# A two-dimensional DFT and a gated feed-forward block: three edits to the weight preparation in the first batch

## The chip, the cores and the metric

The kernel runs on one core of a Trainium2 chip. The metric is the device time of one execution in microseconds (us), median of several runs.

## What is computed

The real part of a two-dimensional DFT over sequence (3008) and width (256) of each of 8 batches, then a feed-forward block of width 2048 with a piecewise gate:

```python
X = np.fft.fft(np.fft.fft(x, axis=1), axis=2).real      # x: 8 x 3008 x 256
h = X @ w_in                                            # 256 x 2048
g = np.where(h >= 1, h, np.where(h <= -1, 0.0, (h + 1) ** 2 / 4))
out = g @ w_out                                         # 2048 x 256
```

The weights arrive as 64-bit floats, and the kernel has to turn their bits into fp32 itself.

## The kernel before

The sequence DFT is split into two stages (`stage1`, `stage2`, with `nyquist` for one column of the width DFT); the width DFT is folded into w_in, so that h comes from one matrix product. All products of the feed-forward block are made in three passes over high and low parts (`wh`, `wl`, `pqh`, `pql`, `gh`, `gl`, `woh`, `wol`).

A **unit** is one block of 128 columns of w_in for one of three column chunks of one batch (16 blocks x 3 chunks x 8 batches). `gemm1` of a unit gives two banks `uv` on TensorE (L359, 6 matmuls); VectorE makes `us` and the two halves of `h` (L362, L364, L365); ScalarE a Relu and a Square into `a` (L372, L373); VectorE the gate (L374); ScalarE its copy `gh` (L375); POOL the rest `gl` (L378). `gemm2` of a unit comes LAG = 4 units later in the code and adds 12 matmuls into four `acc` banks (L402). In batch 0 each chunk has two visits of 8 units: the first ends with the sums copied from `acc` to `o` (L412 on ScalarE, L414 on VectorE) and sent to DRAM, the second adds them. All other batches have one visit of 16 units.

Batch 0 also has to prepare the weights while it runs. There are 16 blocks of weights, **conversions** 0 to 15 (`convert_w`, step "c"): four groups of two blocks of w_in and two of w_out. Conversions 6 to 15 work in the loaded tile `raw` and one PSUM bank `cps`: ScalarE scales the low word into `cps` (L208), VectorE masks the mantissa (L217), adds (L218) and shifts out the exponent (L221), ScalarE takes the exponent's Relu (L222), VectorE its minimum with 255 and the shift to its place (L223), the sign (L224) and the product (L225). Conversions 0 to 5 use other tiles. A **fold** (`fold_w_in` and `fold_delta`, steps "f" and "d") multiplies two converted blocks of w_in by the DFT matrices (L246, L255) and splits the result into `wh` and `wl` (L169, L170). Folds 2 and 3 take their banks from the pool `uv`, which has three and also serves `gemm1`, so the next unit's `gemm1` stands behind them. Units 0 to 7, 8 to 15 and 16 to 23 are the first visits of the three chunks; unit 24 is the first that needs fold 2.

A table `STEPS` says ahead of which unit each preparation step is written. From there a scheduler sets the order on each engine by its own costs and priorities; each engine then runs its queue in order. The FFT of batch 1 starts at unit 25 (FIRST_DFT); POOL adds the two halves of its input x into `y` (L131), which has three buffers, before TensorE's `stage1` matmuls (L270), and ScalarE empties those into `z` (L280).

The lines that the steps of the prediction touch most:

```python
        nc.vector.tensor_scalar(shifted, exp, 255.0, float(1 << 23), op0=ALU.min, op1=ALU.mult)
```

## Time and profile before

| | us |
|---|---|
| median of 3 runs (1764.12 to 1766.73) | 1764.72 |
| the profiled execution | 1765.38 |
| its span | 1763.6 |
| TensorE busy | 1735.8 (98%) |
| VectorE busy | 1440.0 (82%) |
| ScalarE busy | 1346.3 (76%) |
| POOL busy | 1202.1 (68%) |

PE is TensorE's matmuls, DVE is VectorE, ACT is ScalarE, POOL is GpSimd. A share of busy time over the whole span hides that the stretches differ; the rows below are therefore read by stretch. A line number is one of the kernel before.

### The profile page before, as it was taken

How to read it: one execution, taken by the hardware profiler on the slowest of the kernel's cores; microseconds unless marked ns; L12 is line 12 of the kernel's file. 1: busy time of each engine (PE TensorE's matmuls, PEld its weight loads, DVE VectorE, ACT ScalarE, POOL GpSimd, SP SyncE). 2: the span in 40 equal slices, each digit the busy share in tenths (PEclk: the TensorE clock that was granted, in tenths of full speed). 3: DMA queues.
4: the chain of work that ended last, by engine and by line, in shares of the span. 5: the costliest groups of instructions: out<-in, count | busy, mean ns of one | idle time of the engine just before them, and what ended most of it. 6: DMA issues, size and time to landing. Idle time of an engine off the chain costs nothing.

```text
span 1763.6 us, 21942 instructions
## 1 busy us (share of the span) xinstructions
PE 1735.8 (98%) x7982; PEld 1420.5 (81%) x7982; DVE 1440.0 (82%) x1766; ACT 1346.3 (76%) x1580; POOL 1202.1 (68%) x838
## 2 busy tenths in 40 slices
PE   9988999999999999999999999999999999999998
PEld 6766888888888788888888888888888888888877
DVE  6999788888887888878888788878888788888887
ACT  5777877777777877777778877788778787777776
POOL 1545966776768766787667876677676766667775
PEclk9999999999999999999999999999999999999999
DMA  7013321010010100110001100011000000000000
GB/s 230 12 66 101 101 104 60 28 50 30 13 51 28 53 30 1 51 48 33 30 10 51 50 28 24 22 39 50 28 24 34 1 23 32 11 25 5 19 25 24
DMA packets 29963, 72.51 MB, mean 41 GB/s; under 512 B 2976, under 2 KB 8224, under 8 KB 29856
## 3 DMA queue, kind: packets, MB, share of 16 engines
q1 hardware_dynamic: 29568, 70.08, 12.1%
q8 instruction: 62, 1.02, 0.2%
q10 hardware_dynamic: 288, 1.05, 0.2%
q14 instruction: 45, 0.37, 0.1%
HBM read 43.31 MB, written 27.81 MB: 40 GB/s over the span
## 4 chain that ended last, share of the span: by engine, by line
PE 61%; ACT 10%; POOL 9%; issue 6%; DVE 5%; ACTq 0%; POOLq 0%; DVEq 0%
PE acc L402 38%; PE uv L359 19%; POOL gl L378 9%; DVE h L374 4%; ACT a L373 4%; ACT gh L375 3%; ACT a L372 3%; PE s L270 2%; PE s L309 2%; ACT z L280 1%; DVE o L414 0%; DVE h L365 0%; DVE h L364 0%; POOL y L131 0%; ACT o L412 0%
## 5 line engine op out<-in xcount | busy, mean ns | idle before, releaser
L378 POOL TENSOR_TENSOR gl<-h,gh 128x512 fp32r<-128x512 f32 (+1 forms) x765 | 1095.1, 1454 | 513.3 <-ACT gh L375 491.7
L374 DVE SCALAR_TENSOR_TENSOR h<-a,h 128x1024 f32<-128x1024 f32 (+1 forms) x385 | 578.0, 1502 | 219.7 <-ACT a L373 218.1
L375 ACT ACTIVATE gh<-h 128x1024 fp32r<-128x1024 f32 (+1 forms) x385 | 400.6, 1041 | 356.9 <-DVE h L374 344.2
L402 PE MATMUL acc<-gh,woh 128*128 128x512 f32 (+1 forms) x1536 | 608.3, 396 | 6.7 <-ACT gh L375 3.3
L402 PE MATMUL acc<-gl,woh 128*128 128x512 f32 (+1 forms) x1536 | 604.6, 394 | 9.1 <-POOL gl L378 9.1
L402 PE MATMUL acc<-gh,wol 128*128 128x512 f32 (+1 forms) x1536 | 596.2, 388 | 0.0
L372 ACT ACTIVATE a<-h,biases 128x1024 f32<-128x1024 f32 (+1 forms) x385 | 431.7, 1122 | 10.0 <-DVE h L365 7.7
L373 ACT ACTIVATE a<-a 128x1024 f32<-128x1024 f32 (+1 forms) x385 | 398.8, 1036 | 7.1
L402 PEld LDWEIGHTS acc<-gl,woh 128*128 128x128 f32 x1536 | 288.8, 188 | 76.4 <-POOL gl L378 16.8
L402 PEld LDWEIGHTS acc<-gh,woh 128*128 128x128 f32 x1536 | 289.3, 188 | 68.9 <-DVE o L414 5.5
L402 PEld LDWEIGHTS acc<-gh,wol 128*128 128x128 f32 x1536 | 289.5, 188 | 59.2
L364 DVE TENSOR_TENSOR h<-us,uv 128x512 f32<-128x512 f32 (+1 forms) x384 | 259.3, 675 | 67.2 <-POOL gl L378 27.3
L359 PE MATMUL uv<-pqh,wh 128*128 128x512 f32 (+1 forms) x768 | 303.7, 395 | 3.0 <-DVE us L362 2.9
L359 PE MATMUL uv<-pql,wh 128*128 128x512 f32 (+1 forms) x768 | 301.4, 392 | 0.0
L359 PE MATMUL uv<-pqh,wl 128*128 128x512 f32 (+1 forms) x768 | 299.5, 390 | 0.0
L362 DVE SCALAR_TENSOR_TENSOR us<-nyb,delta,uv 128x512 f32<-128x512 f32 (+1 forms) x384 | 278.5, 726 | 14.6 <-PE uv L359 13.8
L365 DVE TENSOR_TENSOR h<-us,uv 128x512 f32<-128x512 f32 (+1 forms) x384 | 256.0, 667 | 0.0
L359 PEld LDWEIGHTS uv<-pqh,wh 128*128 128x128 f32 x768 | 144.4, 188 | 40.9 <-DVE us L362 6.8
L359 PEld LDWEIGHTS uv<-pql,wh 128*128 128x128 f32 x768 | 144.6, 188 | 32.1
L359 PEld LDWEIGHTS uv<-pqh,wl 128*128 128x128 f32 x768 | 144.4, 188 | 30.5 <-issue 0.2
L131 POOL TENSOR_TENSOR y<-x 96x512 f32<-96x512 f32 x60 | 106.4, 1774 | 20.0 <-DMA x<-in_x_dram 8.2
L280 ACT ACTIVATE z<-s 64x192 f32<-64x192 f32 x256 | 86.6, 338 | 6.5 <-PE s L275 1.7
(54 smaller groups left out, 548.0 us busy)
## 6 DMA issues: line engine op xcount, KB each, us to landing
x<-in_x_dram SPq DMA_DIRECT2D x64, 384.0 KB, 3.3
out_dram<-o SPq DMA_DIRECT2D x30, 512.0 KB, 2.8
out_dram<-o SPq DMA_DIRECT2D x16, 482.0 KB, 3.0
nyb<-nyr SPq DMA_DIRECT2D x24, 256.0 KB, 3.4
raw<-in_moe_w_out_dram SPq DMA_DIRECT2D x8, 512.0 KB, 10.9
raw<-in_moe_w_in_dram SPq DMA_DIRECT2D x6, 512.0 KB, 4.5
part<-o SPq DMA_DIRECT2D x4, 512.0 KB, 3.2
o<-part SPq DMA_DIRECT2D x4, 512.0 KB
```

The source lines that it names most:

```text
L131: nc.gpsimd.tensor_tensor(y, t[:, 0], t[:, 1], op=ALU.add)
L280: nc.scalar.activation(dst, src, AF.Copy)
L359: nc.tensor.matmul(t[:, :n], w[m][:, cols], r[:, m, :n], start=(j == 0), stop=(j == 2))
L362: nc.vector.scalar_tensor_tensor(us, nyb[b, k][:, :n], delta[:, f : f + 1], uv[0], op0=ALU.mult, op1=ALU.add)
L364: nc.vector.tensor_tensor(h[:, 0], us, uv[1], op=ALU.subtract)
L365: nc.vector.tensor_tensor(h[:, 1], us, uv[1], op=ALU.add)
L372: nc.scalar.activation(a[:, sl], h[:, sl], AF.Relu, bias=half, scale=0.5)
L373: nc.scalar.activation(a[:, sl], a[:, sl], AF.Square)
L374: nc.vector.scalar_tensor_tensor(h[:, sl], a[:, sl], 1.0, h[:, sl], op0=ALU.min, op1=ALU.max)
L375: nc.scalar.activation(gh[:, sl], h[:, sl], AF.Copy)
L378: eng.tensor_tensor(gl[:, sg], h[:, sg], gh[:, sg].bitcast(F32), op=ALU.subtract)
L402: nc.tensor.matmul(acc[:, :n], w[:, f, wc], g[:, sg], start=(first and j == 0), stop=(last and j == 2))
```

## The change

Three edits. First, in conversions 6 to 15 the minimum with 255 and its scaling by 2^23 go from one VectorE instruction to two ScalarE activations: Relu(255 - e) in place in `raw`, then 255 * 2^23 - 2^23 times it into `cps`; conversions 0 to 5 keep the VectorE instruction. A third constant, 255, joins the biases. Second, all four copies of the sums at the end of a first visit are ScalarE's; before, VectorE took two of them. Third, fold 2 is written ahead of unit 14 and not 13, while conversion 10 and the load of block 12 stay at 13.

```diff
--- before.py
+++ after.py
@@ -79,7 +79,8 @@
     6: "o7 l10",
     9: "c8",
     11: "c9 l11",
-    13: "f2 d2 c10 l12",
+    14: "f2 d2",
+    13: "c10 l12",
     15: "c11 l13",
     17: "o10 c12 l14",
     18: "o11",
@@ -148,10 +149,10 @@
     woh = wts.tile([P, NFT, D], F32R, name="woh")
     wol = wts.tile([P, NFT, D], F32R, name="wol")
     delta = wts.tile([P, NFT], F32, name="delta")
-    biases = wts.tile([P, 2], F32, name="biases")
-    for i, v in enumerate((0.5, -896.0)):
+    biases = wts.tile([P, 3], F32, name="biases")
+    for i, v in enumerate((0.5, -896.0, 255.0)):
         nc.vector.memset(biases[:, i : i + 1], v)
-    half, below = (biases[:, i : i + 1] for i in range(2))
+    half, below, top = (biases[:, i : i + 1] for i in range(3))
 
     def load_cm():
         nc.sync.dma_start(cm, cst[:, _OFF[3] :])
@@ -219,8 +220,12 @@
         if n not in CV:
             exp = low.bitcast(F32)
             nc.vector.tensor_scalar(low, high, 20, 0x7FF, op0=ALU.logical_shift_right, op1=ALU.bitwise_and)
+
             nc.scalar.activation(exp, low, AF.Relu, bias=below)
-        nc.vector.tensor_scalar(shifted, exp, 255.0, float(1 << 23), op0=ALU.min, op1=ALU.mult)
+            nc.scalar.activation(exp, exp, AF.Relu, bias=top, scale=-1.0)
+            nc.scalar.activation(shifted, exp, AF.Copy, bias=255.0 * (1 << 23), scale=-float(1 << 23))
+        else:
+            nc.vector.tensor_scalar(shifted, exp, 255.0, float(1 << 23), op0=ALU.min, op1=ALU.mult)
         nc.vector.scalar_tensor_tensor(shifted, high, 0x80000000, shifted, op0=ALU.bitwise_and, op1=ALU.bitwise_or)
         nc.vector.scalar_tensor_tensor(w, w, 1.0, shifted.bitcast(F32), op0=ALU.add, op1=ALU.mult)
         f32s[n] = w
@@ -408,7 +413,7 @@
                 with tc.high_priority(offset=EVICT_AHEAD):
                     if v:
                         nc.vector.tensor_tensor(dst, acc[:, :n], dst, op=ALU.add)
-                    elif sg:
+                    elif sg or v < visits - 1:
                         nc.scalar.activation(dst, acc[:, :n], AF.Copy)
                     else:
                         nc.vector.tensor_copy(dst, acc[:, :n])
```

The instructions counted in the programs: VectorE 16 fewer (10 minima, 6 copies) and one memset more, ScalarE 26 more. The scheduler's order moves on all engines from unit 3 on. Three places are shown.

ScalarE at conversion 6 (`raw` is its tile, `a` and `gh` belong to units 3 to 5); before:

```order
L372 ACTIVATE a_477<-h_474,biases 128x2x482
L222 ACTIVATE raw_127<-raw_127,biases 128x512
L373 ACTIVATE a_477<-a_477 128x2x482
L375 ACTIVATE gh_478<-h_474 128x2x482
L372 ACTIVATE a_509<-h_506,biases 128x2x482
L169 ACTIVATE woh<-cv_486 128x512
L373 ACTIVATE a_509<-a_509 128x2x482
```

Now:

```order
L377 ACTIVATE a_478<-h_475,biases 128x2x482
L224 ACTIVATE raw_128<-raw_128,biases 128x512
L378 ACTIVATE a_478<-a_478 128x2x482
L225 ACTIVATE raw_128<-raw_128,biases 128x512
L377 ACTIVATE a_511<-h_508,biases 128x2x482
L380 ACTIVATE gh_479<-h_475 128x2x482
L226 ACTIVATE cps_488<-raw_128 128x512
L378 ACTIVATE a_511<-a_511 128x2x482
```

The two new activations stand between the steps of units 3 and 4, one of them ahead of `gh` of unit 3; `woh` moved behind.

TensorE at fold 2 (`wps` and `dps` are the fold's banks, `acc` the second GEMM, `uv` the first GEMM of the next unit, here unit 13); before:

```order
L402 MATMUL acc_0_838<-gh_743,wol 128x512
L246 MATMUL wps_0_854<-cv_685,cm 128x512 x2
L246 MATMUL wps_1_859<-cv_685,cm 128x512 x2
L255 MATMUL dps_864<-cs,cv_685 128x1 x8
L402 MATMUL acc_0_838<-gl_744,woh 128x512
L402 MATMUL acc_1_839<-gh_743,woh 128x512
L402 MATMUL acc_1_839<-gh_743,wol 128x512
L359 MATMUL uv_0_886<-pqh_1_384,wh_69 128x512
```

Now the fold's second half, and the place 23 matmuls of `acc` later where the next `uv` comes, that of unit 14:

```order
L407 MATMUL acc_3_846<-gl_748,woh 128x512
L251 MATMUL wps_0_906<-cv_688,cm 128x512
L251 MATMUL wps_1_911<-cv_688,cm 128x512
L260 MATMUL dps_916<-cs,cv_688 128x1 x7
L407 MATMUL acc_0_843<-gh_793,woh 128x512
```

```order
L407 MATMUL acc_2_845<-gl_836,woh 128x512
L407 MATMUL acc_3_846<-gh_835,woh 128x512
L407 MATMUL acc_3_846<-gh_835,wol 128x512
L364 MATMUL uv_0_926<-pqh_1_385,wh_69 128x512
L364 MATMUL uv_0_926<-pqh_1_385,wl_71 128x512
```

The first GEMM behind the fold moved from 3 `acc` matmuls behind it to 23 behind it, with unit 13 now ahead of the fold.

POOL where the FFT of batch 1 begins (`y_3` is the x half-sum for q = 3, which reuses the buffer of `y_0`; `gl_1304` and `gl_1315` belong to unit 22); before:

```order
L378 TENSOR_TENSOR gl_1195<-h_1190,gh_1194 128x512 x2
L131 TENSOR_TENSOR y_1_1419<-x_1_1240 96x512
L131 TENSOR_TENSOR y_2_1472<-x_2_1242 96x512
L378 TENSOR_TENSOR gl_1261<-h_1256,gh_1260 128x512 x2
L131 TENSOR_TENSOR y_3_1561<-x_3_1244 96x512
L378 TENSOR_TENSOR gl_1304<-h_1299,gh_1303 128x512 x2
L378 TENSOR_TENSOR gl_1338<-h_1333,gh_1337 128x512 x2
```

Now:

```order
L132 TENSOR_TENSOR y_1_1430<-x_1_1250 96x512
L132 TENSOR_TENSOR y_2_1483<-x_2_1252 96x512
L383 TENSOR_TENSOR gl_1271<-h_1266,gh_1270 128x512 x2
L383 TENSOR_TENSOR gl_1315<-h_1310,gh_1314 128x512 x2
L132 TENSOR_TENSOR y_3_1572<-x_3_1254 96x512
L383 TENSOR_TENSOR gl_1349<-h_1344,gh_1348 128x512 x2
```

`gl` of unit 22 moved ahead of `y_3`.

## Rows read from the trace of the kernel before

**Rows 1.** The page's busy tenths in 40 slices of 44 us.

```profile
PE   9988999999999999999999999999999999999998
DVE  6999788888887888878888788878888788888887
ACT  5777877777777877777778877788778787777776
```

**Rows 2.** Busy time of each engine by window, (x) instructions.

```profile
core 0: us, PE busy (x) PEld busy (x) DVE busy (x) ACT busy (x) POOL busy (x), PEclk, DMA share, GB/s
57.00:171.00 114.00, 102.86 (x428) 76.56 (x427) 107.18 (x154) 83.20 (x97) 57.18 (x44) 0.99 0.20 62
171.00:190.00 19.00, 16.92 (x81) 13.54 (x81) 14.58 (x19) 15.32 (x26) 16.21 (x13) 1.00 0.50 152
...
260.00:1763.00 1503.00, 1495.65 (x6884) 1234.65 (x6882) 1219.95 (x1452) 1156.95 (x1318) 1060.12 (x731) 1.00 0.09 31
```

**Rows 3.** The chain that ended last: start us, us, what.

```profile
370.97 2.78 PE acc L402 x12
```

**Rows 4.** Waits from 57 to 190 us: us in total, times, longest us.

```profile
ACT gh L375 <- DVE h L374: 15.4, 12, 2.8
...
PE acc L402 <- POOL gl L378: 7.4, 14, 1.4
...
ACT cps L208 <- DVE cv L225: 5.6, 3, 2.9
...
ACT a L372 <- DVE h L365: 5.1, 6, 2.1
...
PE acc L402 <- ACT gh L375: 3.3, 3, 1.5
...
PE uv L359 <- DVE us L362: 1.9, 2, 1.3
```

**Rows 5.** Groups by line and form, 40 to 190 us: busy us, mean ns | idle before.

```profile
L222 ACT ACTIVATE raw<-raw,biases 128x512 f32<-128x512 uint32 x10 | 7.6, 758 | 1.5 <-DVE raw L221 1.5
...
L223 DVE TENSOR_SCALAR cps<-raw 128x512 uint32<-128x512 f32 x10 | 6.8, 685 | 0.2 <-ACT raw L222 0.2
...
L208 ACT ACTIVATE cps<-raw 128x512 f32<-128x512 uint32 x10 | 6.3, 630 | 5.7 <-DVE cv L225 5.6
...
L414 DVE COPY o<-acc 128x512 f32<-128x512 f32 x4 | 2.7, 684 | 0.0
...
L412 ACT ACTIVATE o<-acc 128x512 f32<-128x512 f32 x4 | 2.3, 586 | 0.6 <-PE acc L402 0.6
```

**Rows 6.** VectorE's timeline: start us, us, what.

```profile
66.51 0.68 DVE L223 TENSOR_SCALAR cps<-raw 128x512 uint32<-128x512 f32 x1
67.10 0.64 DVE L364 TENSOR_TENSOR h<-us,uv 128x482 f32<-128x482 f32 x1
```

**Rows 7.** ScalarE's timeline at one exponent Relu.

```profile
56.05 0.76 ACT L222 ACTIVATE raw<-raw,biases 128x512 f32<-128x512 uint32 x1
56.69 1.00 ACT L373 ACTIVATE a<-a 128x964 f32<-128x964 f32 x1
```

**Rows 8.** Timelines of TensorE and VectorE at the folds [idle before].

```profile
91.97 0.40 PE L359 MATMUL uv<-pql,wh 128*128 128x512 f32 x1
...
103.83 0.40 PE L359 MATMUL uv<-pqh,wh 128*128 128x512 f32 x1
...
104.73 0.75 DVE L362 SCALAR_TENSOR_TENSOR us<-nyb,delta,uv 128x512 f32<-128x512 f32 x1 [2.32 <-PE uv L359]
...
151.59 0.75 DVE L362 SCALAR_TENSOR_TENSOR us<-nyb,delta,uv 128x512 f32<-128x512 f32 x1 [1.31 <-PE uv L359]
...
162.76 0.50 PE L402 MATMUL acc<-gh,woh 128*128 128x512 f32 x1 [1.16 <-ACT gh L375]
```

**Rows 9.** Timelines of POOL and TensorE where batch 1's FFT begins.

```profile
170.01 1.29 POOL L131 TENSOR_TENSOR y<-x 96x512 f32<-96x512 f32 x1 [4.70 <-issue]
171.26 8.94 POOL L378 TENSOR_TENSOR gl<-h,gh 128x512 fp32r<-128x512 f32 x6
...
173.08 0.50 PE L402 MATMUL acc<-gl,woh 128*128 128x512 f32 x1 [1.40 <-POOL gl L378]
...
174.32 0.50 PE L402 MATMUL acc<-gl,woh 128*128 128x512 f32 x1 [0.28 <-POOL gl L378]
```

## The prediction

> **What bounds the kernel now.** Read the page's slices first: TensorE shows 8s and 9s everywhere, and VectorE has its only run of three 9s in slices 2 to 4, about 44 to 176 us [rows 1]. The windows then say which engine is really short in which stretch. From 260 us to the end TensorE is busy 1495.65 of 1503 us, so nothing on the other engines is worth time there [rows 2]. Between 57 and 171 us it is another picture: VectorE is busy 107.18 of 114 us (94%), TensorE 102.86, ScalarE 83.20 (73%) [rows 2]. Twelve matmuls of a later batch take 2.78 us of the chain that ended last, 0.232 us each [rows 3]; 428 in the stretch would be 99 us at most, so TensorE's slack there is larger than its idle time of 11 us. The waits between 57 and 190 us point the same way: ScalarE sits 15.4 us before `gh` for VectorE's `h`, and 5.6 and 5.1 us before its own conversion copy and before `a`, again for VectorE; TensorE waits 7.4 us for `gl`, 3.3 for `gh` and 1.9 for `us` [rows 4]. VectorE sets the pace there, and the kernel after that stretch only shifts with it.
>
> **What the change does in that stretch.** Ten conversions (6 to 15) each lose one VectorE instruction, the minimum and scaling of line 223, and gain two on ScalarE. The six VectorE copies of the first sums in batch 0 (line 414) become ScalarE copies. Later batches have one visit, so their copies stay as they are. TensorE's work is the same.
>
> *VectorE.* A line 223 instruction lasts 685 ns, a copy 684 [rows 5], but instructions overlap at their ends: the next one starts 0.59 us after a line 223 [rows 6]. Four of the six copies lie before 171 us, so 14 x 0.59 = 8.3 us leave the stretch; the other two (1.2 us) leave the stretch after it. VectorE idles only 6.8 us of the 114, so if those waits stay as they are, the stretch shrinks by all of 8.3 us. That is the first term, **-8.3 us**. 107.18 - 8.3 leaves 98.9 us of VectorE work.
>
> *ScalarE.* The trace has no minimum written as two activations. The nearest rows are the exponent's Relu (line 222), in place in the same strided tile with the same kind of bias, 758 ns, next start after 0.64 us, and the copy from that tile into a PSUM bank (line 208), 630 ns [rows 5, 7]. A copy of a sum is 586 ns [rows 5]. So 10 x (0.64 + 0.63) = 12.7 us and 4 x 0.59 = 2.4 us are added, 15.1 in all: ScalarE goes from 83.2 to 98.3 us. What hides it is ScalarE's idle time, 30.8 us in the stretch [rows 2]; between 57 and 190 us it waits 26.1 us for VectorE [rows 4]. It is not free: the queue is in order, and in the new order a minimum's activation stands right ahead of some `gh` or `a`. Zero is one end; the other is all 15.1 us on the path. Since ScalarE still idles about 10% of a shortened stretch, I stay near the lower end and take a tenth, **+1.5 us**.
>
> For one tile of this size the rows show ScalarE no slower than VectorE: 630 ns against 685 into PSUM, 586 against 684 out of it [rows 5]; only the second activation makes the trade uneven, 0.685 us for 1.39. The Trainium skill speaks against the edit: ScalarE: Activation LUTs, Rules for kernel authors, wants relu, minima and multiplications on VectorE, not ScalarE, for its speed per element. The trace does not bear its reason out for these fp32 tiles; with it the edit would be a loss, as in the first rival.
>
> *The folds.* A fold of w_in takes its banks from `uv`, so the next unit's first GEMM stands behind it. Fold 2 in the kernel before has 17 `acc` matmuls of old units between the last `uv` matmul of unit 12 and the first of unit 13 (91.97 to 103.83 us), and VectorE runs dry for 2.32 us at its end; after fold 3 it is 1.31 us [rows 8]. In the new order 39 `acc` matmuls stand in that place at fold 2, and 38 instead of 19 at fold 3: 22 and 19 more, 9.5 us of TensorE work in which VectorE gets nothing new. It has queued work then (`h` of three units, two conversions, the fold's `wl`), some 10 us in about 14 at fold 2 and 7.5 in about 13.4 at fold 3, by the same durations. If VectorE comes there without a backlog its idle time grows by about 0.9 and 4.6 us over the rows just named, 5.5 in all; with a backlog by nothing. I take **+3.0 us**. The first unit behind the fold also has less cover: from unit 21's first matmul to its use in `acc` there are 35 matmuls instead of 45, 8.1 us instead of 10.4, and TensorE already waits 1.16 us at that place [rows 8]; this is the same loss seen from TensorE and is not counted twice.
>
> *POOL.* Before, the fold of x for q = 3 of batch 1 waits for the first FFT matmuls of batch 1 to free a `y` buffer and stands ahead of `gl` of unit 22: POOL sits 4.70 us, six `gl` pile up behind it, and TensorE waits 1.40 and 0.28 us for them [rows 9]. In the new order `gl` of unit 22 goes first; the x fold then precedes `gl` of unit 23, which has 19 matmuls, 4.4 us, as cover for an x fold and a half `gl`, 1.3 us each. That stall should go, **-1.7 us**, or nothing if TensorE then waits for `gh` instead.
>
> *The last two copies* add 1.2 us to ScalarE between 171 and 190 us, where it is busy 15.32 of 19 us [rows 2] and also empties the FFT banks of batch 1. Between 0 and 1.2 us; half, **+0.6 us**.
>
> The third bias memset and the queue position of a weight load cost nothing that the rows let me see: the memset is before any work, and a load is issued whole chunks ahead.
>
> Sum: -8.3 + 1.5 + 3.0 - 1.7 + 0.6 = **-4.9 us**. The profiled run took 1765.38 us (span 1763.6), which gives 1760.5; the median of the timed runs is 0.66 us lower, so 1764.72 - 4.9 = **1759.8 us**.
>
> **Rivals.** (1) *ScalarE becomes the bound: slower.* Its new activations stand ahead of `gh` and `a`, and `gh` is what TensorE and POOL wait for. If all 15.1 us lie on the path and VectorE gives 8.3, the time is 6.8 us longer, about 1771.5. It turns slower when more than about 55% of the 15.1 us lands while somebody waits. Against it stand 26 us of ScalarE's waits for VectorE [rows 4], for it that ScalarE would be busy over 90% of a shortened stretch. 0.12. (2) *The relief is eaten.* Fold stretches at their full 5.5 us and ScalarE at a quarter (3.8) against 8.3: about 1765.7; within 3.5 us of before. For it: both fold stretches in the new order. 0.26. (3) *TensorE becomes the bound.* Its waits there, 7.4 + 3.3 + 1.9 us [rows 4], all go: -12.6, about 1752. VectorE's 98.9 us of work in the 101 that would then be left speak against it. 0.10.
>
> **How the numbers follow.** The forecast, -3.5 to -10 us, has 0.52. A measurement of this kernel can tell about 0.2%, 3.5 us, from no change. Faster by more is forecast plus rival 3, 0.62; within it rival 2, 0.26; slower rival 1, 0.12. For the range: the low end takes the -8.3 and -1.7 with no price at all, -10, and a little of rival 3: 1754.0. The high end takes the folds at 5.5, the activations at 5 and the last copies at 1.2 against 8.3 with no gain on POOL, +3.4: 1768.0. Below lies about 0.08, above about 0.10.
>
> **What would show it.** In the profile after, VectorE should show some 99 us of work in a stretch that ends its conversions 4 to 8 us earlier, ScalarE 98, with its waits for VectorE's `h` well under 15.4 us. TensorE's first batch 1 matmuls should come about 5 us earlier, and everything behind by the same; the batches behind should keep their length. VectorE's wait for `uv` after the folds should be longer than 2.32 and 1.31 us. POOL's 4.70 us idle should be gone. I am wrong if TensorE's waits for `gh` grow past 3.3 us with ScalarE busy right before them (rival 1), or if a wait at units 14 and 21, behind the folds, takes what was won (rival 2).

## The result

The changed kernel takes 1770.51 us (median of 11 runs, 1766.78 to 1773.28), the kernel before beside it 1766.28 us (11 runs). The ratio is 1.0022 with a 95% interval of 1.0012 to 1.0032: **3.9 us slower**, where 4.9 us faster was forecast; the time lies above the range. The profiled execution took 1768.42 us, with a span of 1766.6 us beside 1763.6.

In the changed kernel lines move down by one to five: L222 is the shift (L221 before), L218 the mask (L217), L224 the exponent's Relu, L225 and L226 the two new activations, L229 and L230 sign and product, L364 and L407 the GEMMs, L367 `us`, L369 and L370 the halves of `h`, L377 to L380 `a`, gate and `gh`, L383 `gl`, L132 the x sum, L275 the stage 1 matmuls, L285 and L288 their way into `z`, L417 the copies of the sums.

Busy time by window after the change; it answers to [rows 2]:

```profile
core 0: us, PE busy (x) PEld busy (x) DVE busy (x) ACT busy (x) POOL busy (x), PEclk, DMA share, GB/s
57.00:171.00 114.00, 102.04 (x417) 74.70 (x416) 104.04 (x138) 94.86 (x120) 59.75 (x44) 0.99 0.20 61
171.00:190.00 19.00, 17.93 (x90) 14.45 (x89) 14.60 (x19) 16.56 (x27) 14.65 (x11) 1.00 0.48 156
...
260.00:1763.00 1503.00, 1498.89 (x6903) 1238.40 (x6901) 1223.95 (x1458) 1158.50 (x1320) 1064.46 (x733) 1.00 0.09 31
```

From 57 to 171 us VectorE is busy 104.04 us, only 3.1 less than before, with 16 fewer instructions; ScalarE is busy 94.86, 11.7 more. TensorE got through 417 matmuls there instead of 428. Behind 260 us the pace is the same: 1498.89 us busy with 19 matmuls more, which are those that had been delayed. The waits between 57 and 190 us answer to [rows 4]:

```profile
ACT gh L380 <- DVE h L379: 7.2, 7, 2.2
DVE h L369 <- POOL gl L383: 6.6, 6, 1.9
ACT a L377 <- DVE h L370: 6.2, 4, 2.5
PE acc L407 <- ACT gh L380: 6.1, 5, 2.0
PE acc L407 <- POOL gl L383: 4.6, 12, 0.7
POOL y L132 <- DMA x<-in_x_dram: 4.5, 2, 4.0
DVE us L367 <- PE uv L364: 3.0, 5, 0.9
...
POOL y L132 <- PE s L275: 2.2, 1, 2.2
```

and two rows of the kernel before, for VectorE:

```profile
DVE us L362 <- PE uv L359: 5.8, 7, 2.3
DVE h L364 <- POOL gl L378: 3.6, 2, 2.4
```

ScalarE waits less for VectorE (7.2 instead of 15.4 us before `gh`), so VectorE's relief did arrive there. But TensorE now waits 6.1 us for `gh` instead of 3.3; what it saved on `gl` (4.6 instead of 7.4) went there. VectorE itself stands idle longer, 10.0 us of the 114 from 57 to 171 us instead of 6.8. From 57 to 190 us its waits for POOL's `gl` grew from 3.6 to 6.6 us, while those for `uv` fell from 5.8 to 3.0.

**Where VectorE's gain went.** The groups of the conversions by form, 40 to 190 us, of the changed kernel:

```profile
L222 DVE TENSOR_SCALAR raw<-raw 128x512 uint32<-128x512 uint32 x10 | 9.7, 970 | 0.0
L218 DVE TENSOR_SCALAR cv<-raw 128x512 uint32<-128x512 uint32 x10 | 8.2, 832 | 0.0
L224 ACT ACTIVATE raw<-raw,biases 128x512 f32<-128x512 uint32 x10 | 7.6, 763 | 1.9 <-DVE raw L222 1.9
L225 ACT ACTIVATE raw<-raw,biases 128x512 f32<-128x512 f32 x10 | 7.6, 760 | 0.0
...
L226 ACT ACTIVATE cps<-raw 128x512 uint32<-128x512 f32 x10 | 6.2, 622 | 0.1
```

and the same shift and mask in the kernel before:

```profile
L217 DVE TENSOR_SCALAR cv<-raw 128x512 uint32<-128x512 uint32 x10 | 7.3, 735 | 0.0
...
L221 DVE TENSOR_SCALAR raw<-raw 128x512 uint32<-128x512 uint32 x10 | 5.3, 533 | 0.0
```

The change does not touch the shift, and yet its ten cost 9.7 us instead of 5.3. VectorE's and POOL's timelines at two of them in the changed kernel, one slow, one quick, show why:

```profile
126.97 1.52 DVE L222 TENSOR_SCALAR raw<-raw 128x512 uint32<-128x512 uint32 x1
...
116.75 0.42 DVE L222 TENSOR_SCALAR raw<-raw 128x512 uint32<-128x512 uint32 x1
```

```profile
103.12 9.53 POOL L383 TENSOR_TENSOR gl<-h,gh 128x512 fp32r<-128x512 f32 x6 [4.48 <-ACT gh L380]
121.74 2.75 POOL L383 TENSOR_TENSOR gl<-h,gh 128x512 fp32r<-128x512 f32 x2 [9.09 <-ACT gh L380]
126.89 3.99 POOL L383 TENSOR_TENSOR gl<-h,gh 128x512 fp32r<-128x512 f32 x3 [2.40 <-ACT gh L380]
...
126.89 1.31 POOL L383 TENSOR_TENSOR gl<-h,gh 128x512 fp32r<-128x512 f32 x1 [2.40 <-ACT gh L380]
```

The one at 126.97 starts while POOL is at `gl` (126.89 to 130.88) and takes 1.52 us; the one at 116.75 lies between two groups of `gl` (112.65 to 121.74) and takes 0.42. The last row is the first of the three `gl` at 126.89, by itself: it ends at 128.20, and the shift 0.29 us later. This holds for every slow one. Of the twenty masks and shifts, 13 begin while an instruction of POOL runs and take longer than 0.42 us (7 in the kernel before), and each of them ends 0.28 to 0.29 us after the end of an instruction of POOL. One that begins first stays at 0.42 us, even if POOL begins while it runs. The median shift grew from 0.42 to 0.97 us: in the new order VectorE comes to it more often while POOL is at work. The Trainium skill, SBUF — State Buffer, SBUF: two separate sides, says that GpSimd and some kinds of VectorE instructions lock a shared pair of ports for a whole instruction, so that the later one waits for the other's end; these rows agree with that.

**Where batch 1's FFT begins.** POOL's 4.70 us ahead of `gl` of unit 22 [rows 9] are gone, as forecast. Two other waits came, on POOL's timeline of the changed kernel, ahead of the x sums for q = 1 and q = 5:

```profile
160.73 2.70 POOL L132 TENSOR_TENSOR y<-x 96x512 f32<-96x512 f32 x2 [4.01 <-DMA x<-in_x_dram]
...
189.05 2.12 POOL L132 TENSOR_TENSOR y<-x 96x512 f32<-96x512 f32 x1 [2.15 <-PE s L275]
```

The last conversion's product starts at 169.27 us, 6.6 us later than before (162.67), and the input tiles of batch 1 use the conversions' buffers. TensorE then waits for `z`:

```profile
183.52 1.13 PE L275 MATMUL s<-cs,y 96*128 96x96 f32 x8 [0.80 <-ACT z L288]
...
200.68 2.02 PE L275 MATMUL s<-cs,y 96*128 96x96 f32 x8 [2.26 <-ACT z L285]
...
202.96 0.61 PE L407 MATMUL acc<-gh,wol 128*128 128x482 f32 x1
203.36 0.61 PE L407 MATMUL acc<-gl,woh 128*128 128x482 f32 x1
...
207.56 0.39 PE L364 MATMUL uv<-pqh,wl 128*128 128x512 f32 x1
207.79 0.39 PE L364 MATMUL uv<-pql,wh 128*128 128x512 f32 x1
```

Behind the 2.26 us the matmuls start 0.40 us apart, and from 207.56 on again 0.23: the granted clock between 200 and 207 us is 0.53, that is mostly the lower of TensorE's two levels (1.2 and 2.4 GHz). At the start of unit 25's second GEMM the changed kernel is 0.5 us behind the kernel before, at unit 29's 4.4. Seven us at 0.53 cost about 3.3 us by themselves (7 x 0.47, an estimate), so in this trace most of the 3.9 us between the two units is time at the lower level. That made the FFT the first suspect.

### The profile page after: what moved, and what is told of

Its sections match the earlier page's. It is cut to its first block, busy times and chain, and to the rows that moved or that the text cites. A ratio compares the mean times of both kernels' runs of the same rounds, so it can differ in the third digit from the quotient of the medians.

```text
span 1766.6 us, 21942 instructions
## 1 busy us (share of the span) xinstructions
PE 1738.0 (98%) x7982; PEld 1422.5 (81%) x7982; DVE 1438.0 (81%) x1751; ACT 1360.3 (77%) x1606; POOL 1205.0 (68%) x838
## 4 chain that ended last, share of the span: by engine, by line
PE 67%; ACT 11%; POOL 9%; issue 7%; DVE 6%; DMA 0%; ACTq 0%; POOLq 0%; DVEq 0%
PE acc L407 41%; PE uv L364 20%; POOL gl L383 8%; DVE h L379 5%; ACT a L378 4%; ACT gh L380 3%; PE s L275 3%; ACT a L377 3%; PE s L314 2%; ACT z L285 1%; PE wps L251 1%; PE warm L430 0%; POOL y L132 0%; DVE h L370 0%; DVE h L369 0%
## 5 line engine op out<-in xcount | busy, mean ns | idle before, releaser
L383 POOL TENSOR_TENSOR gl<-h,gh 128x512 fp32r<-128x512 f32 (+1 forms) x765 | 1099.2, 1460 | 514.9 <-ACT gh L380 487.9
L380 ACT ACTIVATE gh<-h 128x1024 fp32r<-128x1024 f32 (+1 forms) x385 | 400.6, 1041 | 350.2 <-DVE h L379 317.7
L407 PE MATMUL acc<-gh,woh 128*128 128x512 f32 (+1 forms) x1536 | 609.0, 397 | 9.2 <-ACT gh L380 6.1
L407 PE MATMUL acc<-gl,woh 128*128 128x512 f32 (+1 forms) x1536 | 604.9, 394 | 6.5 <-POOL gl L383 6.2
L407 PE MATMUL acc<-gh,wol 128*128 128x512 f32 (+1 forms) x1536 | 597.4, 389 | 0.0
L377 ACT ACTIVATE a<-h,biases 128x1024 f32<-128x1024 f32 (+1 forms) x385 | 431.5, 1122 | 11.2 <-DVE h L370 9.1
L407 PEld LDWEIGHTS acc<-gl,woh 128*128 128x128 f32 x1536 | 289.1, 188 | 74.3 <-POOL gl L383 14.9
L407 PEld LDWEIGHTS acc<-gh,woh 128*128 128x128 f32 x1536 | 289.8, 189 | 71.4 <-ACT gh L380 8.4
L407 PEld LDWEIGHTS acc<-gh,wol 128*128 128x128 f32 x1536 | 290.0, 189 | 59.9 <-DVE wol L171 0.3
L369 DVE TENSOR_TENSOR h<-us,uv 128x512 f32<-128x512 f32 (+1 forms) x384 | 259.6, 676 | 69.0 <-POOL gl L383 28.8
L364 PE MATMUL uv<-pqh,wh 128*128 128x512 f32 (+1 forms) x768 | 303.4, 395 | 2.8 <-DVE us L367 1.4
L364 PE MATMUL uv<-pql,wh 128*128 128x512 f32 (+1 forms) x768 | 301.8, 393 | 0.0
L364 PE MATMUL uv<-pqh,wl 128*128 128x512 f32 (+1 forms) x768 | 299.6, 390 | 0.0
L367 DVE SCALAR_TENSOR_TENSOR us<-nyb,delta,uv 128x512 f32<-128x512 f32 (+1 forms) x384 | 278.9, 727 | 17.9 <-PE uv L364 17.3
L370 DVE TENSOR_TENSOR h<-us,uv 128x512 f32<-128x512 f32 (+1 forms) x384 | 256.2, 667 | 0.0
L364 PEld LDWEIGHTS uv<-pqh,wh 128*128 128x128 f32 x768 | 144.5, 188 | 39.6 <-DVE h L370 5.4
L364 PEld LDWEIGHTS uv<-pql,wh 128*128 128x128 f32 x768 | 144.7, 188 | 32.0
L364 PEld LDWEIGHTS uv<-pqh,wl 128*128 128x128 f32 x768 | 144.5, 188 | 30.9 <-issue 0.2
L132 POOL TENSOR_TENSOR y<-x 96x512 f32<-96x512 f32 x60 | 105.5, 1758 | 19.3 <-DMA x<-in_x_dram 11.4
L285 ACT ACTIVATE z<-s 64x192 f32<-64x192 f32 x256 | 86.7, 339 | 6.5 <-PE s L280 2.2
## 6 DMA issues: line engine op xcount, KB each, us to landing
raw<-in_moe_w_out_dram SPq DMA_DIRECT2D x8, 512.0 KB, 10.7
```

What stands on the lines that cost most here:

```text
L132: nc.gpsimd.tensor_tensor(y, t[:, 0], t[:, 1], op=ALU.add)
L285: nc.scalar.activation(dst, src, AF.Copy)
L364: nc.tensor.matmul(t[:, :n], w[m][:, cols], r[:, m, :n], start=(j == 0), stop=(j == 2))
L367: nc.vector.scalar_tensor_tensor(us, nyb[b, k][:, :n], delta[:, f : f + 1], uv[0], op0=ALU.mult, op1=ALU.add)
L369: nc.vector.tensor_tensor(h[:, 0], us, uv[1], op=ALU.subtract)
L370: nc.vector.tensor_tensor(h[:, 1], us, uv[1], op=ALU.add)
```

## The experiments

All runs have the kernel before beside them on the same chip. How much time TensorE spends at its lower level differs from run to run and by kernel. Of 137 runs of the kernel before, those with a mean granted clock of 0.998 took 1762.6 us (median of 11), of 0.997 1764.9 (84), of 0.996 1767.0 (40); two were at 0.995. A mean of 0.001 less is 3.5 us more at the lower level; a straight line through these runs gives 0.56 us of time for each of them. The last two columns of the table split the mean difference by that: what the different time at the lower level accounts for, and the rest, **at equal clock**. I put the rest's uncertainty at about 1 us. Whether a kernel's own waits bring a part of the time at the lower level about is not settled, so the medians are kept beside it. no_fold_move and after_dft26 have 6 runs, before_y47 has 8, the others 10 to 12.

| kernel | median us | before | ratio (95%) | by clock | at equal clock |
|---|---|---|---|---|---|
| changed kernel | 1770.51 | 1766.28 | 1.0022 (1.0012 to 1.0032) | +0.4 | +3.9 |
| copies_only | 1765.03 | 1765.16 | 0.9996 (0.9986 to 1.0006) | -0.9 | +0.1 |
| min_only | 1764.46 | 1765.16 | 0.9997 (0.9988 to 1.0005) | -2.2 | +1.6 |
| fold_only | 1765.15 | 1765.16 | 1.0002 (0.9993 to 1.0010) | -1.1 | +1.0 |
| no_fold_move | 1772.15 | 1765.16 | 1.0038 (1.0025 to 1.0050) | +2.1 | +4.4 |
| no_copies | 1764.85 | 1764.83 | 1.0002 (0.9993 to 1.0011) | -0.6 | +0.9 |
| no_min | 1764.67 | 1764.83 | 1.0003 (0.9994 to 1.0012) | +0.2 | -0.1 |
| fused_all | 1764.73 | 1764.83 | 1.0004 (0.9995 to 1.0013) | +1.1 | -0.7 |
| fused_only | 1762.08 | 1764.83 | 0.9985 (0.9976 to 0.9994) | -1.7 | -1.1 |
| after_dft26 | 1773.32 | 1766.03 | 1.0047 (1.0029 to 1.0064) | +2.5 | +5.2 |
| before_dft26 | 1764.43 | 1766.03 | 0.9998 (0.9988 to 1.0008) | -0.8 | 0.0 |
| nfm_dft26 | 1769.84 | 1766.03 | 1.0021 (1.0012 to 1.0030) | 0.0 | +3.9 |
| after_xo | 1769.60 | 1765.86 | 1.0019 (1.0010 to 1.0028) | -1.0 | +4.1 |
| before_xo | 1768.04 | 1765.86 | 1.0011 (1.0002 to 1.0019) | +1.9 | -0.1 |
| after_y47 | 1768.03 | 1765.86 | 1.0017 (1.0008 to 1.0025) | -0.5 | +3.1 |
| before_y47 | 1769.34 | 1765.86 | 1.0022 (1.0012 to 1.0032) | +3.0 | +0.6 |
| after_k01 | 1766.89 | 1766.01 | 1.0007 (0.9998 to 1.0016) | -1.4 | +2.3 |
| after_k2 | 1766.42 | 1766.01 | 1.0003 (0.9994 to 1.0012) | +1.3 | -0.5 |

The changed kernel's clock part is against the mean of the 137 runs.

### One edit at a time, and two without the third

Theory T: the copies on ScalarE lose the time. S: ScalarE's minima do. F: the later fold does. **copies_only**, against the kernel before:

```diff
-                    elif sg:
+                    elif sg or v < visits - 1:
```

> Only the two copies per chunk of the first sums move to ScalarE; minima and fold 2 stay as before. Theory T (the change loses its time where the FFT of batch 1 begins, because POOL's x half-sum of q = 5 waits for TensorE ahead of gl of unit 26, and that order comes from the copies): 2 to 5 us slower than before, the start of unit 28's second GEMM at least 13 us after that of unit 26 (10.4 before, 15.7 in the change), and up to unit 25 within 1 us of before. Theory S (ScalarE's twenty added activations cost the time): within 1 us of before. Theory F (the later fold costs it): within 1 us of before.

**min_only**, against the kernel before (with the third bias):

```diff
-        nc.vector.tensor_scalar(shifted, exp, 255.0, float(1 << 23), op0=ALU.min, op1=ALU.mult)
+            nc.scalar.activation(exp, exp, AF.Relu, bias=top, scale=-1.0)
+            nc.scalar.activation(shifted, exp, AF.Copy, bias=255.0 * (1 << 23), scale=-float(1 << 23))
+        else:
+            nc.vector.tensor_scalar(shifted, exp, 255.0, float(1 << 23), op0=ALU.min, op1=ALU.mult)
```

> Only the minima of conversions 6 to 15 move to ScalarE. Theory T: unit 28 starts 10 to 11 us after unit 26, as before; the conversions give the gain that VectorE's 6 us of freed work leaves after ScalarE's 13 us, so 0 to 4 us faster. Theory S: 3 to 6 us slower, with the loss before unit 25. Theory F: 2 to 5 us faster.

**fold_only**, against the kernel before:

```diff
-    13: "f2 d2 c10 l12",
+    14: "f2 d2",
+    13: "c10 l12",
```

> Only fold 2 is written ahead of unit 14 instead of 13. Theory T and theory S: within 1.5 us of before, and units 26 to 28 as before. Theory F: 3 to 6 us slower, with TensorE's wait at unit 13 or 14, behind the fold.

**no_fold_move**, against the changed kernel: the diff just shown, undone.

> The change with fold 2 back ahead of unit 13: minima and copies are ScalarE's. Theory T: POOL's order is another one here (the half-sum of q = 4 ahead of gl of unit 24, that of q = 5 ahead of gl of unit 26), TensorE's FFT matmuls of q = 2 come as late as in the change; the loss between units 26 and 28 is smaller than in the change, 0 to 3 us, and the total lies between before and the change. Theory S: as slow as the change, 3 to 6 us over before. Theory F: 2 to 6 us faster than before.

All three theories fall: by the medians no edit alone is slower than before (at equal clock min_only is 1.6 us behind, less than Theory S wants). Minima and copies together are 7 us slower, and with the later fold, forecast as a price of 3 us, it is 4. The two remaining pairs came next, and a form in which VectorE gets its relief for nothing, because it leaves out the minimum with 255. **no_copies**, against the changed kernel:

```diff
-                    elif sg or v < visits - 1:
+                    elif sg:
```

> The minimum on ScalarE and the later fold, with the first sums' copies as before: the change without its second edit. Theory L (the two ScalarE activations lengthen each conversion, its input tiles come free later, and only together with the copies on ScalarE does that delay reach TensorE): without the copies little of the loss is left, so -2 to +1 us against before. Rival S (ScalarE's minima cost time by themselves and the fold adds its part): +2 to +5 us, about as the full change. Rival C (the copies alone are what TensorE waits behind): cannot be told from L here, the next run does that.

**no_min**, against the changed kernel: the diff of min_only, undone.

> The first sums' copies on ScalarE and the later fold, with the minimum on VectorE as before: the change without its first edit. Theory L: the conversions keep their length, so 0 to -3 us against before. Rival C (copies on ScalarE are the loss as soon as VectorE's order shifts): +2 to +4 us. Rival P (copies and the later fold are a bad pair, the minima play no part): also +2 to +4 us, with the TensorE clock of the stretch after 200 us below 0.9 as in the full change.

**fused_only**, against the kernel before:

```diff
-    for i, v in enumerate((0.5, -896.0)):
+    for i, v in enumerate((0.5, -896.0, -896.0 * (1 << 23))):
...
-            exp = low.bitcast(F32)
...
-            nc.scalar.activation(exp, low, AF.Relu, bias=below)
-        nc.vector.tensor_scalar(shifted, exp, 255.0, float(1 << 23), op0=ALU.min, op1=ALU.mult)
+            nc.scalar.activation(shifted, low, AF.Relu, bias=top, scale=float(1 << 23))
+        else:
+            nc.vector.tensor_scalar(shifted, exp, 255.0, float(1 << 23), op0=ALU.min, op1=ALU.mult)
```

> As the run before this one (minimum left out, scaling taken into the exponent's Relu) with the copies and the fold as in the kernel before: ten VectorE instructions fewer and nothing added. Theory L, and the prediction's first term (10 x 0.59 us): 2 to 6 us below before. Rival N (VectorE is not what sets the pace of this stretch): within 1 us of before.

**fused_all** is this edit with the copies and the later fold of the change.

> The full change, but the minimum with 255 is left out in conversions 6 to 15 and the scaling by 2^23 is taken into the exponent's Relu, which writes the PSUM bank directly: VectorE loses the same ten instructions as in the change, and ScalarE gains none. Theory L (the price of the change is the longer conversion on ScalarE): conversions should end about 7 to 10 us earlier than in the change, batch 1's input should come no later than before, and the time should be 3 to 8 us below before. Rival N (VectorE is not what sets the pace, so taking its instructions away is worth nothing): within 1 us of before, conversions earlier or not. Rival P (the copies with the later fold lose the time): 2 to 4 us above before.

Both pairs are as fast as before, so rivals C and P fall: only minima **and** copies lose time. fused_only is 2.75 us faster by the medians, the one form faster than before, with less than half of the 5.9 us that ten instructions of 0.59 us should give. At equal clock it is 1.1, hardly outside the 1 us of rival N, so that rival N is weakened rather than gone. Theory L has its numbers in the pairs and in fused_only, but not in fused_all. The conversions of fused_only, the slowest of its shifts, and its window from 57 to 171 us:

```profile
L220 DVE TENSOR_SCALAR raw<-raw 128x512 uint32<-128x512 uint32 x10 | 7.3, 726 | 0.0
L221 ACT ACTIVATE cps<-raw,biases 128x512 uint32<-128x512 uint32 x10 | 7.2, 717 | 2.1 <-DVE cv L218 1.7 <-DVE raw L220 0.4
...
L217 DVE TENSOR_SCALAR cv<-raw 128x512 uint32<-128x512 uint32 x10 | 6.5, 649 | 0.0
```

```profile
151.03 3.06 DVE L220 TENSOR_SCALAR raw<-raw 128x512 uint32<-128x512 uint32 x1
```

```profile
57.00:171.00 114.00, 103.61 (x439) 77.43 (x438) 104.81 (x147) 85.66 (x103) 63.66 (x48) 1.00 0.22 69
```

The ten shifts are stretched here too, 7.3 instead of 5.3 us, with nothing added to ScalarE; that is mostly the one at 151.03, which stands behind three of POOL's instructions. Its last product starts at 158.66 us, 4.0 earlier than before, and TensorE has 439 matmuls done by 171 us instead of 428. The difference to min_only is what the twenty activations cost: about 2 us by the medians (2.75 - 0.7), 2.7 at equal clock, of 13.8 us that they are busy (L225 and L226 of the changed kernel). fused_all was to be 3 to 8 us faster and is as before. It is 2.65 us behind fused_only by the medians, 3.2 by the means, of which 2.8 is time at the lower level.

### The FFT of batch 1

Theory M: the loss arises at units 26 to 28, where POOL's x sum for q = 5 stands ahead of a `gl`. C: it arises in the conversions. **after_again** is the changed kernel once more.

> The changed kernel itself, for a second trace. Theory M (the weight stretch comes out about even and the loss arises where batch 1's FFT meets units 26 to 28, because POOL's x sum for q = 5 stands ahead of a gl and ScalarE's z behind it): the second GEMM of unit 25 starts within 1.5 us of before (188.6 us), TensorE waits about 2 us for z near 200 us, the clock then stands at the lower level for some us, and unit 29 is 3 to 6 us behind before. Theory C (the loss is in the conversions' own stretch, and the wait near 200 us was chance of one execution): unit 25 is already 3 us or more behind, or no wait near 200 us is seen.

One run, 1774.77 us. The wait is there again, for 2.2 us at 206.32, behind the same 2.15 us on POOL:

```profile
206.32 1.13 PE L275 MATMUL s<-cs,y 96*128 96x96 f32 x8 [2.22 <-ACT z L285]
```

```profile
194.70 2.12 POOL L132 TENSOR_TENSOR y<-x 96x512 f32<-96x512 f32 x1 [2.15 <-PE s L275]
```

No lower level followed it this time, and unit 25 was already 6.2 us behind, with lower levels in the first 150 us. From there to unit 29 it lost another 2.4 us, at the full clock. So the wait belongs to the kernel, and the spell that came with it in the first trace was that execution's. **before_dft26** and **after_dft26** start the FFT a unit later, in both kernels; **nfm_dft26** does so in no_fold_move:

```diff
-FIRST_LOAD, FIRST_DFT = 21, 25
+FIRST_LOAD, FIRST_DFT = 21, 26
```

> The changed kernel with batch 1's FFT beginning one unit later (26 instead of 25), which puts POOL's x sum for q = 5 behind gl of unit 27 and not ahead of gl of unit 26. Nothing in the weight preparation is edited. Theory M: the loss of the change goes, so within 1.5 us of the next run, its control. Theory C: 3 to 5 us above the control.

> The kernel before with the same later beginning of batch 1's FFT: the control of the run above. Both theories: within 2 us of before, the FFT only has one unit less to hide under.

> The minima and the copies on ScalarE with fold 2 in its old place (which was 7 us slower than before) and batch 1's FFT one unit later. Its POOL order had no x sum for q = 5 ahead of gl of unit 26, and batch 1's input landed 7 us later there. Theory M in its wide form (what loses the time is the meeting of late input and a FFT that starts too early): within 2 us of the control. Theory C (the pair of edits loses the time in the conversions): still 5 to 8 us above it.

The control stays, the changed kernel is still 7.3 us above before, and nfm_dft26 3.8. Against the control they are 8.9 and 5.4 us slower. Theory M falls in both forms: moved or not, the loss stays. Next came the late input (X) against POOL's queue (Q). **after_xo** and **before_xo** put two input tiles into buffers that nobody uses then:

```diff
-        tag, bufs = ("xt", 4) if b or q < 4 else ("gl", 4) if q < 7 else ("o", 2)
+        tag, bufs = ("o", 2) if b == 1 and q < 2 else ("xt", 4) if b or q < 4 else ("gl", 4) if q < 7 else ("o", 2)
```

> The changed kernel with the first two input tiles of batch 1 in the two buffers of the sums' copies, which lie idle from about 135 to 178 us, so that they need not wait for the conversions' tiles. TensorE's order and POOL's order from gl of unit 21 on stay word for word. Theory X (late input is the cause): POOL's waits for x, 4.5 us, go, and the time falls by 3 to 5 us, to that of the next run. Theory Q (POOL's queue at units 26 to 31 is the cause): TensorE's wait of about 2.2 us near 200 us stays and the time stays 3 to 5 us above the next run.

> The kernel before with the same two input tiles in the same buffers: the control of the run above. Its input was hardly late (POOL waits 1.2 us for x between 57 and 215 us), so both theories: within 1 us of before.

**after_y47** and **before_y47** let the later x sums go into their own input tile:

```diff
-            y = sb.tile([96, CH], F32, tag="y", name=f"y_{b}_{q}", bufs=3)
+            y = t[:, 0] if b == 1 and q > 3 else sb.tile([96, CH], F32, tag="y", name=f"y_{b}_{q}", bufs=3)
```

> The changed kernel with the x sums for q = 4 to 7 of batch 1 written into their own input tile instead of a y buffer. Nothing is left that an x sum waits for but its input, and no x sum stands in POOL's queue between gl of units 25 and 29. TensorE's order stays word for word. Theory Q: the 2.15 us POOL wait, the 3.6 us VectorE wait behind it and TensorE's 2.2 us near 200 us go, 2 to 5 us less than the changed kernel. Theory X: the input is still late, so the time stays within 1 us of the changed kernel's 4 above before.

> The kernel before with the same x sums in place: the control of the run above. TensorE waits 1.14 us near 205 us and 1.40 us near 173 us there, behind the same queue: Theory Q 0 to 2 us below before, Theory X within 1 us.

X falls: in the trace of after_xo none of POOL's 4.5 us of waits for x between 57 and 215 us is left, and the time is 3.7 us above before all the same. Q fares little better: the 2.2 us wait went (the longest for `z` is 1.00 us), but only 0.8 us at equal clock with it. Both controls were slower than forecast, so that by the medians after_xo is only 1.6 us above its control, and after_y47 is 1.3 below its own. X and Q therefore fall by the column at equal clock, not by the medians. In before_y47 an x sum in POOL's queue waits 4.07 us for its input, TensorE waits 3.63 us for the `gl` behind it, and the window from 166 to 173 us has a granted clock of 0.53:

```profile
164.85 1.27 POOL L131 TENSOR_TENSOR x<-x 96x512 f32<-96x512 f32 x1 [4.07 <-DMA x<-in_x_dram]
...
167.90 0.79 PE L402 MATMUL acc<-gl,woh 128*128 128x512 f32 x1 [3.63 <-POOL gl L378]
170.10 0.79 PE L402 MATMUL acc<-gl,woh 128*128 128x512 f32 x1 [1.41 <-POOL gl L378]
```

### The copies, split

Theory Z: the last two copies, ahead of `z`, lose the time; W: the weight stretch does, wherever the copies stand. In the changed kernel's ScalarE queue all four copies at the end of unit 23 and a `gh` come ahead of the last pieces of `z` for q = 0:

```profile
178.01 0.60 ACT L417 ACTIVATE o<-acc 128x512 f32<-128x512 f32 x1 [0.65 <-PE acc L407]
178.50 1.00 ACT L378 ACTIVATE a<-a 128x964 f32<-128x964 f32 x1
179.40 1.27 ACT L417 ACTIVATE o<-acc 128x512 f32<-128x512 f32 x2
180.69 0.34 ACT L285 ACTIVATE z<-s 64x192 f32<-64x192 f32 x1
181.05 0.60 ACT L417 ACTIVATE o<-acc 128x512 f32<-128x512 f32 x1
182.15 1.01 ACT L380 ACTIVATE gh<-h 128x964 fp32r<-128x964 f32 x1 [0.50 <-DVE h L379]
183.07 0.40 ACT L288 ACTIVATE z<-s 64x24 f32<-64x24 f32 x2
```

TensorE's next stage 1 group, at 183.52, stands right behind them; before, it ran at 179.90. **after_k01** gives the last two copies back to VectorE, **after_k2** moves only those (the line `k < 2` becomes `k == 2`):

```diff
-                    elif sg or v < visits - 1:
+                    elif sg or (v < visits - 1 and k < 2):
```

> The changed kernel, with the last two of the six moved copies (end of unit 23, third chunk) on VectorE as before; the four earlier ones, the minima and the fold stay as changed. In its order z for q = 0 of batch 1 comes ahead of the second copy of unit 23 and of gh of unit 25. Theory Z (the loss is these two copies ahead of z, which hold the FFT's one bank): the loss goes, -1.5 to +1.5 us against before, and TensorE's second stage 1 group of batch 1 starts about 179 to 181 us. Theory W (the weight stretch loses the time, wherever the copies stand): 3 to 5 us above before.

> The complement: the changed kernel with only the last two copies (end of unit 23) moved to ScalarE and the four earlier ones on VectorE as before. From z on ScalarE's and POOL's orders are those of the change. Theory Z: 3 to 5 us above before, the second stage 1 group after 182 us and TensorE waiting about 2 us for z near 200 us. Theory W: within 1.5 us of before, since fewer copies load ScalarE in the weight stretch.

Theory Z is half right. Without the last two copies the group starts at 180.79, the 2.2 us wait is gone, and most of the loss with it by the medians (+0.9 us left); at equal clock only 1.6 of the 3.9 us go, and 2.3 stay. But after_k2 has the group at 185.82 and the wait as Z said, and is as fast as before: that wait alone costs nothing that can be measured.

```profile
202.95 1.32 PE L275 MATMUL s<-cs,y 96*128 96x96 f32 x6 [2.24 <-ACT z L285]
```

TensorE's waits of more than 0.1 us on its timeline from 171 to 215 us add up to 3.4 us before, 3.4 in the changed kernel, 4.2 in after_k2 and 2.8 in after_k01: the long one largely takes the place of the 1.40 and 1.14 us that the kernel before has there. Theory W falls as well.

**What stays open.** By the medians the loss needs the minima, the four earlier copies and the two last ones together: without any one of the three it is 0 to 0.9 us. At equal clock this holds for the minima and the four earlier copies (-0.5 to +0.9); without the two last ones 2.3 of the 3.9 us stay. No single wait carries the loss. In the two traces of the changed kernel the time that TensorE spends beyond its matmuls, away from the lower level (sum of the distances between starts, less the usual distance of a matmul of that size), grows from about 24 us before to about 25 and 27 between units 3 and 34, and no stretch carries that in both.

One part of it shows in the groups of mask and shift, whose twenty instructions no edit touches. Together they take 12.7 us in the kernel before and 10.7 to 14.7 in the other kernels that lose 1.6 us or less at equal clock. They take 15.1 and 15.2 in nfm_dft26 and no_fold_move, and 17.8 to 18.6 in the changed kernel, after_dft26, after_k01, after_xo and after_y47, all of which lose 2.3 us or more. The one exception is fused_all, with 17.5 us and no loss, and of the kernels with 15 us or more it is the only one without the twenty activations. So the slow kernels are those in which POOL holds VectorE up most while ScalarE has the activations too. That is a parallel and no proof: no run took the meetings away alone. Each variant also has its own order from the scheduler on every engine, so what the table gives an edit includes that order; no run moved one of the three edits with the order held. Why the parts cost so much less than the whole was not settled.

## Why the prediction was wrong, step by step

- **VectorE sets the pace there: half right, and the term (-8.3) was mis-sized. This is the step that failed first.** Ten minima taken from VectorE for nothing gave 2.75 us of 5.9 by the medians and 1.1 at equal clock (fused_only). The six copies, of which four made 2.4 us of the term, gave nothing net of what they cost ScalarE (copies_only). The failed sentence is "if those waits stay as they are, the stretch shrinks by all of 8.3 us". Neither waits nor durations stayed. VectorE's work from 57 to 171 us fell by 3.1 us, not 8.3: the ten shifts grew by 4.4 us and the ten masks by 0.9 beside POOL (the shifts by 2.0 in fused_only). Its idle time there grew by 3.1 us, most of all before `h`, for POOL's `gl`. So TensorE is 11 matmuls behind at 171 us, where it was to be ahead. A busy share of 94% did not mean that each microsecond taken away shortens the stretch.
- **ScalarE (+1.5): right in kind, too small.** Twenty activations cost 2 to 2.7 us (min_only against fused_only), 15 to 20% of their busy time rather than a tenth. What the sum left out is that the two edits do not add up: minima alone cost 1.6 us at equal clock, copies alone 0.1, both 4.4. ScalarE's waits for VectorE before `gh`, which were to hide the activations, fell from 15.4 to 7.2 us; that they no longer sufficed for both is likely but not shown.
- **The folds (+3.0): wrong.** By its own rounded figures the upper bound is 6.3 us and not 5.5 (14 - 10 - 2.32 = 1.7 at fold 2, not 0.9), which matters little, since even 3.0 was too much. VectorE's waits for `uv` between 57 and 190 us fell from 5.8 to 3.0 us, none longer than 0.9, where they were to exceed 2.32 and 1.31. fold_only is 0.0 us by the medians and 1.0 at equal clock, and beside minima and copies the later fold costs nothing either (no_fold_move against the changed kernel: some 3 us gained by the medians, 0.5 at equal clock).
- **POOL (-1.7): the wait went, the gain did not come.** The 4.70 us ahead of `gl` of unit 22 vanished as described; 4.01 us for x and 2.15 for a `y` buffer came two sums earlier and two later. Lateness of the input was not thought of, though the conversions' longer chain on ScalarE was in the diff. It cost little by itself (after_xo, at equal clock).
- **The last copies (+0.6): the right place, too small.** They count at equal clock for 1.6 of 3.9 us (changed kernel against after_k01), by the medians for 3.3, though without the four earlier ones they cost nothing (after_k2). The queue position was right ("also empties the FFT banks of batch 1"), the price was taken from ScalarE's busy time alone and not from who waits for `z`.
- **Rival 1** gave 1771.5 and came within 1 us. Its sign that it is so, TensorE's waits for `gh` growing past 3.3 us, is there (6.1). That its number is so near is luck: 15 to 20% of the activations' time is paid, where it has all of ScalarE's added 15.1 us on the path, and of the 8.3 us that it lets VectorE give most did not come. Nor is it the reason that the Trainium skill gives in ScalarE: Activation LUTs, Rules for kernel authors, speed per element, which it states for bf16: here, per tile, ScalarE is about as fast (622 and 760 ns, L226 and L225, against 685 for the minimum on VectorE), but it needs two.
- **Clock.** The sum was made at one level. TensorE's time at the lower one differs between kernels by up to 3 us of their time either way, which is as large as most terms; nothing in the sum allowed for it.

## What to carry to other kernels

Price an offload by a variant in which the relief is free: here that gave 1.1 to 2.75 us of the 5.9 that the busy times promised, and the activations' 2 to 2.7 us left little or nothing of it. Look at an instruction's single durations and not at its mean: 0.42 and 1.52 us in one group pointed to meetings with another engine, and a new order changes how many there are. Two edits that load the same engine can cost more than their sum, so run pairs as well as singles. Where a difference of some microseconds is at stake, set the granted clock of each run beside its time before the cause is sought in waits.

## What the runs showed of the hardware

- The same VectorE shift (128 x 512, uint32, SBUF to SBUF) lasts 0.42 us alone and up to 1.52 us when POOL is at `gl`; behind three of POOL's instructions in a row it took 3.06 (fused_only). A slow one ends 0.28 to 0.29 us after the end of an instruction of POOL. Moving other work on VectorE decides how often it meets POOL (5.3 us in ten before, 9.7 in the changed kernel).
- An activation of ScalarE that reads the strided integer tile, scales, clips below and writes integers into PSUM lasts 717 ns, not more than the 758 ns of the plain in-place Relu.
- Runs of one kernel differ by 3 to 9 us, and in the kernel before their mean granted clock goes along: 1762.6 us at 0.998, 1767.0 at 0.996. Waits of TensorE of 2 to 4 us sometimes came with a stretch at 0.53 (200 to 207 us in the first trace of the changed kernel, 166 to 173 in before_y47) and sometimes, at the same place of the same kernel, not (after_again).
